# Scores of two query tiles issued in one go, and the first chunks loaded and ordered anew, in an attention and channel-mix kernel

## Chip, core and metric

The kernel runs on one core of a Trainium2 chip. The metric is device microseconds of one execution. PE is TensorE (matrix products), DVE VectorE, ACT ScalarE, POOL GpSimd, and SP SyncE, whose queue issues all DMA here.

## What is computed

Eight batches, eight heads, 576 queries, head width 64. Keys and values are mean-pooled by eight, so each head has 72 keys. The attention output, 4608 rows of 512, goes through a gated channel mix:

```python
k_p = k.reshape(B, H, Sp, pool, D).mean(axis=3)      # Sp = 72
scores = scale * np.matmul(q, k_p.transpose(0, 1, 3, 2))
attn = np.exp(scores - np.max(scores, axis=-1, keepdims=True))
attn = attn / (np.sum(attn, axis=-1, keepdims=True) + 1e-09)
x = matmul(attn, v_p)                                # heads joined: 8 x 576 x 512
xk = mu_k * x + (1.0 - mu_k) * x_prev                # x_prev: one row earlier
xr = mu_r * x + (1.0 - mu_r) * x_prev
k = np.maximum(xk @ w_k, 0.0)                        # 512 -> 1024
v = k * k @ w_v                                      # 1024 -> 512
r = 1.0 / (1.0 + np.exp(-(xr @ w_r)))
return (r * v).astype(np.float32)
```

## The kernel before

The 4608 rows are cut into 36 **tiles** of 128 queries and 13 **chunks** (128, 256, then eleven of 384 rows, three tiles each). Attention works by tile, the channel mix by chunk.

For a tile, `softmax` takes the PSUM tile `sc` (two banks; there is one such tile) and calls `part`. From tile 3 on (`ROWS_FROM`) the scores are 16 products of 64x72 with 64 rows and 64 columns of the array each (L710), so that four stand in the array side by side; each is two PE records in the profile, 32 for a tile. DVE takes the row maxima (L743) and subtracts them (L760), after which `sc` is free (`emptied`); ACT takes the exponential (L766), DVE sums, and DVE or POOL scales into `px` and `pm` (L781, L786, by the table `NORM_BY`). `transposed` (four transposes, L821) and `transposed_rest` (one, L868) turn the result, each in one bank of the kind `bank`. There are three such banks, and three of the kind `mm`.

For a chunk, `quarters` multiplies by the values (L897, L905) into `sc` and two of the kind `bank`; `shifted` and `joined` (L998) mix each row with the one before it; `x_parts` splits the result into two float32r halves (`xkh`, `xkl`, `xrh`, `xrl`: L1020 on ACT, L1022 on POOL). Then `hidden` (L1048: eight groups of 12 products of 384 columns), `gate` (L1097: three groups of 12 of 512) and `mixed` (L1130: three groups of 24 of 512) run on banks of the kind `mm`; DVE multiplies the mix by the gate (`rs`, L1140).

Chunks 0 and 1 run on whole float32 weights while the weights arrive. Each of the 20 weight blocks (eight of `w_k`, four of `w_r`, eight of `w_v`, 512 KB each) is loaded (L478) as raw 64-bit words, rebuilt into float32 by `convert` (ACT L519, DVE L521 and L524), and cut into two float32r parts by `split` (ACT L546, DVE or POOL L549). Key and value loads go through staging buffers (L502), of which the first chunks have few: `stage_103` is handed from `k0` to `v0`, `k2`, `k3`, `v3` or `v2`, and so on, each load waiting until the sums of the one before (L556, L598, L567) are done. `LOADS` is the order in which SP issues the first loads; a load that waits holds back all behind it.

No engine's order is written out by hand. Each piece of work is a generator in `Order`, with a due time plus a correction from the table `EARLIER`; while the program is built, a list scheduler with costs for each step picks the next piece, and that order is fixed in the program.

Of the kernel before, what the change touches and what calls it, by code (L numbers as in the profile page):

```python
# [38 lines left out]
WHOLE_ATT = (0, 1)  # L39
TWICE = 3  # L40
PACKED = (0, 1)
SPREAD_ON_ACT = (0, 1)
HALVED = (0,)
EARLY = (("sl", 2), ("xrl", 1))

REBASE = 2.0 ** -((1023 - 127) // 8)

LOADS = (
    "k0 wk0 c0 r1 k1 r0 q0 q2 q1 v0 wk1 v1 q5 q3 k2 wk2 wk3 q4 k3 wk4 v3 wk5 wk6 wk7 wr0 wr1 v2 wr2 "
    "wr3 wv2 wv0 wv1 wv3 wv4 wv5 wv6 wv7 "  # L50
)

SUM_BY = {"k0": "t", "k1": "v", "v0": "t", "v1": "t", "r0": "g", "k2": "g", "k3": "v", "v2": "g", "v3": "v", "r1": "v"}

NORM_BY = {0: 'g', 1: 'v', 2: 'v', 3: 'v', 4: 'g', 6: 'g', 5: 'v', 7: 'v'}
WARMING = 4
FILLERS = 40

LOW_BY = {"k": "gvgvvvgv", "r": "gvgv", "v": "gvvgvvgv"}
BY_HEAD = ((0, 1),)  # L60

ROWS_FROM = 3
BESIDE = (1,)
SQUARED_ON_ACT = (8, 0)
COPIES_ON_ACT = ()

EARLIER = {
# [42 lines left out]
}  # L110
PLAN = ""
SPARE = 0.5
# [137 lines left out]
def attention_then_channel_mix(  # L250
# [15 lines left out]
    order = Order()  # L266
    need = lambda *what: ("need", *what)
    take = lambda kind: ("take", kind)
# [82 lines left out]
    for tag, n in EARLY:  # L351
        t = sb.tile([P, n, 2 * POOL * KEYS], F32, name=f"early_{tag}", tag=tag)
# [16 lines left out]
    def stretches(at, n):  # L369
# [9 lines left out]
    tiles = [  # L379
        (c, o, stretches(a + o, P)) for c, (a, n) in enumerate(zip(starts, CHUNKS)) for o in range(0, n, P)  # L380
    ]
# [61 lines left out]
    held = {}  # L443
# [183 lines left out]
    def last_values(b):  # L627
# [34 lines left out]
        order.give("vq", vq)  # L662
        order.make(("rest", b))

    def softmax(i):

        parts = tiles[i][2]
        if i:
            yield need(("scoring", i - 1))
            c = tiles[max(i - 2, 0)][0] - 1  # L670
            if c >= 0 and c not in WHOLE_ATT:
                yield need(("attended", c, 0))
        yield need(("q", i), *[("keys", b, p) for b, *_ in parts for p in range(1 if i in HALVED else 2)])
        pair = None
        if i in BESIDE:
            pair = [(yield take("mm")), (yield take("mm"))]
            sc = None
            halves = [t.rearrange("p (a n) -> p a n", a=1) for t in pair]
        else:
            sc = yield take("sc")  # L680
            halves = [sc[:, a:a + 1] for a in range(2)]
        held["halves", i] = sc, pair, halves
        if i in HALVED:
            for kind in ("mx", "e", "sm", "px", "pm"):
                held[kind, i] = yield take(kind)
        order.make(("scoring", i))
        if i in HALVED:
            yield from part(i, 0, 1)
        else:
            yield from part(i, 0, 2)  # L690
# [3 lines left out]
            held[kind, i] = yield take(kind)  # L694
        return held[kind, i]

    def part(i, a0, a1):
        parts, na, rows = tiles[i][2], a1 - a0, i >= ROWS_FROM
        mine = slice(a0, a1)
        yield need(("scoring", i))  # L700
        sc, pair, halves = held["halves", i]
        yield need(*[("keys", b, p) for b, *_ in parts for p in range(a0, a1)])
        qs = held["q", i]
        yield "pe", 0.86 if rows else (1.0 if len(parts) == 1 else 1.14) * na / 2, False
        if rows:
            for g in range(NPAIR):
                for b, _, n, o in [(b, 0, D, o + d) for b, _, n, o in parts for d in range(0, n, D)]:
                    for a in range(2):
                        r, k = slice(a * D, (a + 1) * D), g * KEYS
# [5 lines left out]
        for g in range(2 * a0, 2 * a1) if not rows else ():  # L715
            k = (g % 2) * 2 * KEYS
            for b, _, n, o in parts:
# [1 line left out]
                    out=halves[g // 2][o:o + n, 0, k:k + 2 * KEYS],  # L719
                    lhsT=qs[:, g, o:o + n], rhs=kbd[b % 2][:, g, :], start=True, stop=True,  # L720
                )
        order.make(("scores", i, a0))

        def emptied():
            order.make(("emptied", i, a0))
            if pair:
                for a in range(a0, a1):
                    order.give("mm", pair[a])

        if na == 1:  # L730
            svs = [halves[a0]]
# [3 lines left out]
        n = 8 * KEYS // 2 * na  # L735
# [42 lines left out]
        v = NORM_BY.get(i, "g") == "v"  # L778
# [465 lines left out]
```

## Time and profile before

| | |
|---|---|
| three runs | 624.78, 624.91, 625.52 us; median 624.91 |
| the profiled execution | 624.51 us |
| its span | 622.7 us |
| PE busy | 612.5 us, 98% of the span |
| DVE, ACT, POOL busy | 59%, 56%, 34% |
| DMA queue of the loads and stores | 22.7% of 16 engines' span |

A busy share says how long an engine had at least one instruction in flight. Matrix products overlap, so PE's pace is read from the distance between two starts in the timeline rather than from a duration. The span is 1.8 us shorter than the execution's own time.

### The profile page before, as it was taken

How to read it: one execution, taken by the hardware profiler on the slowest of the kernel's cores; microseconds unless marked ns; L12 is line 12 of the kernel's file. 1: busy time of each engine (PE TensorE's matmuls, PEld its weight loads, DVE VectorE, ACT ScalarE, POOL GpSimd, SP SyncE). 2: the span in 40 equal slices, each digit the busy share in tenths (PEclk: the TensorE clock that was granted, in tenths of full speed). 3: DMA queues.
4: the chain of work that ended last, by engine and by line, in shares of the span. 5: the costliest groups of instructions: out<-in, count | busy, mean ns of one | idle time of the engine just before them, and what ended most of it. 6: DMA issues, size and time to landing. Idle time of an engine off the chain costs nothing.

```text
span 622.7 us, 10827 instructions
## 1 busy us (share of the span) xinstructions
PE 612.5 (98%) x4175; PEld 515.6 (83%) x4175; DVE 368.1 (59%) x730; ACT 351.1 (56%) x759; POOL 210.5 (34%) x333
## 2 busy tenths in 40 slices
PE   8999999999999999999999999999999999999997
PEld 7986448879879879977978978977887987987986
DVE  5999888776457366566636736737735735623411
ACT  4678847766656537636627636645654653655320
POOL 0432286066043039128216107405604303405000
PEclk9999999999999999999999999999999999999999
DMA  8467622331014211052011411033001100000001
GB/s 309 171 235 254 245 103 79 124 129 35 18 49 147 60 52 52 1 204 69 1 52 63 157 52 47 7 123 126 24 17 52 35 1 35 18 1 34 18 0 52
DMA packets 19011, 50.56 MB, mean 81 GB/s; under 512 B 2256, under 2 KB 2512, under 8 KB 18960
## 3 DMA queue, kind: packets, MB, share of 16 engines
q1 hardware_dynamic: 18960, 49.87, 22.7%
q8 instruction: 33, 0.54, 0.4%
q14 instruction: 18, 0.15, 0.1%
HBM read 40.43 MB, written 9.44 MB: 80 GB/s over the span
## 4 chain that ended last, share of the span: by engine, by line
PE 80%; DVE 6%; POOL 5%; DMA 4%; ACT 2%; issue 2%; SPq 0%; POOLq 0%; DVEq 0%; ACTq 0%
PE mm L1048 29%; PE mm L1130 24%; PE mm L1097 15%; PE sc L710 3%; PE bank L821 2%; POOL xkl L1022 2%; DMA stage<-in_kT 2%; DMA got_wv<-in_w_v 1%; PE bank L431 1%; DVE stage L556 1%; POOL xrl L1022 1%; PE sc L905 1%; DMA got_wk<-in_w_k 1%; DVE kbd L598 1%; PE mm L567 1%
## 5 line engine op out<-in xcount | busy, mean ns | idle before, releaser
L1048 PE MATMUL mm<-xkh,w_k 128*128 128x384 f32 x704 | 180.8, 337 | 2.1 <-DVE rs L1140 1.1
L1130 PE MATMUL mm<-w_v,sh 128*128 128x512 f32 x528 | 173.1, 398 | 0.0
L1048 PEld LDWEIGHTS mm<-xkh,w_k 128*128 128x128 f32 x704 | 125.9, 188 | 4.0 <-ACT xkh L1020 1.6
L1130 PEld LDWEIGHTS mm<-w_v,sh 128*128 128x128 f32 x528 | 99.1, 188 | 26.9 <-issue 5.0
L1048 PE MATMUL mm<-xkl,w_k 128*128 128x384 f32 x352 | 118.0, 335 | 0.9 <-POOL xkl L1022 0.9
L1130 PE MATMUL mm<-w_v,sl 128*128 128x512 f32 x264 | 103.3, 391 | 0.0
L781 POOL TENSOR_TENSOR px<-e,sm 128x64 f32<-128x64 f32 (+1 forms) x32 | 11.2, 350 | 261.4 <-DVE sm L775 197.7
L1097 PE MATMUL mm<-w_r,xrh 128*128 128x512 f32 x264 | 85.2, 395 | 0.0
L1073 DVE TENSOR_TENSOR sl<-rk,sh 128x384 fp32r<-128x384 f32 x88 | 54.2, 617 | 34.7 <-ACT sh L1071 34.7
L1071 ACT CAST sh<-rk 128x384 fp32r<-128x384 f32 x88 | 45.2, 514 | 47.7 <-DVE rk L1065 47.2
L1048 PEld LDWEIGHTS mm<-xkl,w_k 128*128 128x128 f32 x352 | 66.1, 188 | 1.6 <-POOL xkl L1022 1.6
L743 DVE TENSOR_REDUCE mx<-sc 128x8 f32<-128x576 f32 (+1 forms) x36 | 26.4, 735 | 57.7 <-PE sc L710 57.0
L1065 DVE SCALAR_TENSOR_TENSOR rk<-mm,rk 128x384 f32<-128x384 f32 x88 | 48.7, 553 | 17.6 <-ACT rk L1058 17.2
L1022 POOL TENSOR_TENSOR xkl<-xm,xkh 128x384 fp32r<-128x384 f32 x44 | 44.3, 1016 | 43.7 <-ACT xkh L1020 39.8
L1097 PEld LDWEIGHTS mm<-w_r,xrh 128*128 128x128 f32 x264 | 49.6, 188 | 10.2
L1130 PEld LDWEIGHTS mm<-w_v,sl 128*128 128x128 f32 x264 | 49.6, 188 | 9.3
L1058 ACT ACTIVATE rk<-mm 128x384 f32<-128x384 f32 x88 | 42.9, 489 | 22.1 <-PE mm L1048 18.9
L556 POOL TENSOR_TENSOR stage<-stage 128x512 f32<-128x512 f32 (+7 forms) x59 | 52.6, 898 | 2.2 <-DVE pr L848 0.3
L1097 PE MATMUL mm<-w_r,xrl 128*128 128x512 f32 x132 | 51.5, 390 | 0.0
L766 ACT ACTIVATE e<-e 128x576 f32<-128x576 f32 (+1 forms) x36 | 24.4, 679 | 46.4 <-DVE e L760 46.0
L1140 DVE TENSOR_TENSOR rs<-mm,rs 128x512 f32<-128x512 f32 x36 | 24.7, 685 | 41.6 <-PE mm L1130 41.5
L1022 POOL TENSOR_TENSOR xrl<-xm,xrh 128x384 fp32r<-128x384 f32 x44 | 44.4, 1019 | 0.6 <-ACT xrh L1020 0.3
(143 smaller groups left out, 909.7 us busy)
## 6 DMA issues: line engine op xcount, KB each, us to landing
qs<-in_qT SPq DMA_DIRECT2D x36, 256.0 KB, 3.1
out<-rs SPq DMA_DIRECT2D x36, 256.0 KB, 2.0
stage<-in_kT SPq DMA_DIRECT2D x15, 576.0 KB, 4.7
stage<-in_vm SPq DMA_DIRECT2D x15, 512.0 KB, 3.8
got_wk<-in_w_k SPq DMA_DIRECT2D x8, 512.0 KB, 5.3
got_wv<-in_w_v SPq DMA_DIRECT2D x8, 512.0 KB, 10.4
stage<-in_vr SPq DMA_DIRECT2D x6, 384.0 KB, 3.6
got_wr<-in_w_r SPq DMA_DIRECT2D x4, 512.0 KB, 7.5
```

The source lines that it names most:

```text
L556: nc_eng.tensor_tensor(out=st[:, :, :w], in0=st[:, :, :w], in1=st[:, :, w:2 * w], op=ALU.add)
L743: nc.vector.tensor_reduce(out=by_bank(mx)[:, o], in_=sv, axis=AX.X, op=ALU.max)
L766: nc.scalar.activation(out=e[:, mine], in_=e[:, mine], func=AF.Exp, scale=scale)
L1022: nc.gpsimd.tensor_tensor(out=lo, in0=xm[:, :n], in1=hi, op=ALU.subtract)
L1048: nc.tensor.matmul(out=hp, lhsT=w[:, o], rhs=x[:, ct, :n], start=(ct == 0 and k == 0), stop=(ct == NCT - 1 and k == len(terms) - 1),)
L1058: nc.scalar.activation(out=rk[:, :n], in_=hp, func=AF.Relu)
L1065: nc.vector.scalar_tensor_tensor(out=rk[:, :n], in0=hp, scalar=0.0, in1=rk[:, :n], op0=ALU.max, op1=ALU.mult)
L1071: nc.scalar.copy(out=sh[:, :n], in_=rk[:, :n])
L1073: nc.vector.tensor_tensor(out=operand("sl", c)[:, jt, :n], in0=rk[:, :n], in1=sh[:, :n], op=ALU.subtract)
L1097: nc.tensor.matmul(out=bank, lhsT=x[:, ct, o], rhs=w, start=(ct == 0 and k == 0), stop=(ct == NCT - 1 and k == len(terms) - 1),)
L1130: nc.tensor.matmul(out=bank, lhsT=s[:, o], rhs=w, start=(jt == 0 and k == 0), stop=(jt == NJT - 1 and k == len(terms) - 1),)
L1140: nc.vector.tensor_tensor(out=rs, in0=bank, in1=rs, op=ALU.mult)
```

## The change

Two things. First, from tile 9 on (`PAIRS_FROM`) tiles go in pairs, (9, 10), (11, 12) and so on to (33, 34), with tile 35 alone. The first of a pair takes `sc` and also two of the three tiles of the kind `bank`, waits until the tile before the pair is emptied and both query loads and all keys are there, and then issues the scores of both, the second tile's into the two banks. The second tile's `part` starts at the maxima, by bank: two maxima and two subtractions of 288 columns in place of one each of 576.

Second, `LOADS` and nearly all of `EARLIER` have new values, and some steps of the first chunks change their engine: spreading the last values (L651 on ACT to L656 on DVE), six copies of L848 to ACT, three squares from ACT to DVE, one set of sums from POOL to DVE, the norm of tile 7 from DVE to POOL.

```diff
-SPREAD_ON_ACT = (0, 1)
+SPREAD_ON_ACT = ()
 LOADS = (
-    "k0 wk0 c0 r1 k1 r0 q0 q2 q1 v0 wk1 v1 q5 q3 k2 wk2 wk3 q4 k3 wk4 v3 wk5 wk6 wk7 wr0 wr1 v2 wr2 "
-    "wr3 wv2 wv0 wv1 wv3 wv4 wv5 wv6 wv7 "
+    "k0 c0 k1 wk0 r0 q0 r1 q1 wk1 q5 wk2 v1 v0 q2 q4 wk3 k2 q3 wk4 k3 wk5 wk6 wk7 v3 wr0 wr1 wr2 wr3 "
+    "wv2 wv0 wv1 wv3 wv4 wv5 v2 wv6 wv7 "
 )
-SUM_BY = {..., "r0": "g", ..., "v2": "g", ..., "r1": "v"}
+SUM_BY = {..., "r0": "t", ..., "v2": "v", ..., "r1": "g"}
+PAIRS_FROM = 9
-SQUARED_ON_ACT = (8, 0)
-COPIES_ON_ACT = ()
+SQUARED_ON_ACT = (5, 0)
+COPIES_ON_ACT = (1, 2, 3, 4)
 EARLIER = {
-    "filling": 493.7, "last_values 1": 512.3, "convert k 0": 153.8, "split k 0": -68.2, ...
+    "filling": 417.4, "last_values 1": 487.3, "convert k 0": 480.0, "split k 0": 222.7, ...
...
+    def leads(i):
+        return i >= PAIRS_FROM and (i - PAIRS_FROM) % 2 == 0 and i + 1 < len(tiles)
     def softmax(i):
+        if leads(i - 1):
+            yield need(("scores", i, 0))
+            yield from part(i, 0, 2)
+            return
...
+        if leads(i):
+            yield need(
+                ("emptied", i - 1, 0), ("q", i + 1), *[("keys", b, p) for b, *_ in tiles[i + 1][2] for p in range(2)]
+            )
+            pair = [(yield take("bank")), (yield take("bank"))]
+            held["halves", i + 1] = None, pair, [t.rearrange("p (a n) -> p a n", a=1) for t in pair]
+            order.make(("scoring", i + 1))
...
     def part(i, a0, a1):
+        if not leads(i - 1):
...
+            scores(i, a0, a1)
+            if leads(i):
+                scores(i + 1, 0, 2)
+                order.make(("scores", i + 1, 0))
```

Three places show what this does to the order of instructions; line numbers in the changed file are 1 to 27 higher.

On PE in chunk 2, before: the scores of tiles 9 and 10 stand in `sc` one after the other, with products of the gate between them.

```order
L710 MATMUL sc_110<-kbd_68,qs_102 64x72 x16
L1097 MATMUL mm_115<-w_r_772,xrh_850 128x512
...
L821 MATMUL bank_112<-ident,pm_88 128x128 x4
...
L710 MATMUL sc_110<-kbd_68,qs_101 64x72 x16
L1097 MATMUL mm_115<-w_r_828,xrh_850 128x512
```

On PE in chunk 2, now (L721 is L710 before); the two bank rows alternate, 16 in all:

```order
L1124 MATMUL mm_116<-w_r_819,xrh_850 128x512
L721 MATMUL sc_110<-kbd_68,qs_100 64x72 x16
L721 MATMUL bank_111<-kbd_68,qs_101 64x72
L721 MATMUL bank_112<-kbd_68,qs_101 64x72
...
L1124 MATMUL mm_116<-w_r_888,xrh_850 128x512
```

The 32 products of two tiles now follow each other without anything between them.

On PE in the mix of chunks 0 and 1, before: `got_wv_667` is the seventh block of `w_v` to be rebuilt, and its first product stands behind a tile's scores and the quarters of chunk 2.

```order
L1130 MATMUL mm_115<-got_wv_641,stage_105 128x512
L710 MATMUL sc_110<-kbd_69,qs_102 64x72 x16
...
L897 MATMUL sc_110<-ptr_614,vbd_r_73 128x192 x2
...
L1130 MATMUL mm_115<-got_wv_663,stage_105 128x512
L1130 MATMUL mm_115<-got_wv_667,stage_105 128x512
```

There now (L1157 is L1130 before); the seventh block is `got_wv_703`:

```order
L1157 MATMUL mm_115<-got_wv_547,sh_478 128x512
...
L848 MATMUL bank_111<-ident,pm_88 128x128 x4
L1157 MATMUL mm_115<-got_wv_703,sh_478 128x512
L721 MATMUL sc_110<-kbd_69,qs_100 64x72 x16
L1157 MATMUL mm_115<-got_wv_708,sh_478 128x512
...
L924 MATMUL sc_110<-ptr_638,vbd_r_73 128x192 x2
```

Its first product now stands ahead of those scores and of the quarters.

On SP's queue, before: `v2` (the first row here) stands ahead of two `w_r` and all eight `w_v` blocks.

```order
L502 DMA stage_103<-in_vm 128x1024
L478 DMA got_wr_619<-in_w_r 128x1024
L478 DMA got_wr_627<-in_w_r 128x1024
L478 DMA got_wv_635<-in_w_v 128x1024
...
L478 DMA got_wv_676<-in_w_v 128x1024
```

There now (L503 and L479 are L502 and L478 before):

```order
L479 DMA got_wv_540<-in_w_v 128x1024
L479 DMA got_wv_547<-in_w_v 128x1024
L503 DMA stage_103<-in_vm 128x1024
L479 DMA got_wv_703<-in_w_v 128x1024
L479 DMA got_wv_708<-in_w_v 128x1024
```

Only the seventh and eighth block stand behind it now.

## Rows read from the trace of the kernel before

**Rows 1.** The page: busy time and share of the span, and the clock in 40 slices
```profile
PE 612.5 (98%) x4175; PEld 515.6 (83%) x4175; DVE 368.1 (59%) x730; ACT 351.1 (56%) x759; POOL 210.5 (34%) x333
...
PEclk9999999999999999999999999999999999999999
```

**Rows 2.** Busy time by stretch, us (instructions), for the whole program
```profile
0.00:95.50 95.50, 91.75 (x637) 67.18 (x637) 78.47 (x174) 65.46 (x158) 38.38 (x70) 1.00 0.60 215
95.50:600.00 504.50, 501.84 (x3457) 433.14 (x3458) 287.58 (x554) 284.57 (x600) 172.11 (x264) 1.00 0.17 58
```

**Rows 3.** Waits of PE: line and tile, waited for: us in total, times, longest
```profile
PE mm L1048 <- DVE rs L1140: 1.1, 1, 1.1
PE mm L1048 <- ACT xkh L1020: 1.0, 2, 0.5
PE mm L1048 <- POOL xkl L1022: 0.9, 2, 0.5
PE sc L718 <- ACT e L752: 0.7, 1, 0.7
PE bank L821 <- DVE xm L998: 0.5, 1, 0.5
```

**Rows 4.** Timeline of PE round one tile's scores: start us, us, instruction
```profile
169.83 0.39 PE L1097 MATMUL mm<-w_r,xrl 128*128 128x512 f32 x1
170.06 0.39 PE L1097 MATMUL mm<-w_r,xrh 128*128 128x512 f32 x1
170.38 0.73 PE L710 MATMUL sc<-kbd,qs 64*64 64x72 f32 x32
171.04 0.50 PE L1130 MATMUL mm<-w_v,sh 128*128 128x512 f32 x1
171.38 0.40 PE L1130 MATMUL mm<-w_v,sl 128*128 128x512 f32 x1
```

**Rows 5.** The same scores seen through two narrower windows
```profile
170.56 0.56 PE L710 MATMUL sc<-kbd,qs 64*64 64x72 f32 x24
...
170.87 0.24 PE L710 MATMUL sc<-kbd,qs 64*64 64x72 f32 x4
```

**Rows 6.** Timeline of PE round the four transposes of one tile
```profile
184.27 0.39 PE L1130 MATMUL mm<-w_v,sh 128*128 128x512 f32 x1
184.50 0.60 PE L821 MATMUL bank<-ident,pm 128*128 128x128 f32 x4
...
185.17 0.40 PE L1130 MATMUL mm<-w_v,sl 128*128 128x512 f32 x1
```

**Rows 7.** Groups of DVE by form: xcount | busy us, mean ns | idle before
```profile
L760 DVE TENSOR_TENSOR e<-sc,mx 128x576 f32<-128x576 f32 x34 | 25.7, 755 | 1.2
...
L743 DVE TENSOR_REDUCE mx<-sc 128x8 f32<-128x576 f32 x34 | 25.5, 751 | 57.1 <-PE sc L710 57.0
...
L743 DVE TENSOR_REDUCE mx<-mm 128x4 f32<-128x288 f32 x2 | 0.9, 449 | 0.0
L760 DVE TENSOR_TENSOR e<-mm,mx 128x288 f32<-128x288 f32 x2 | 0.9, 435 | 0.0
```

**Rows 8.** Timeline of DVE: the conversions of the seventh and eighth w_v blocks
```profile
72.96 1.28 DVE L524 SCALAR_TENSOR_TENSOR got_wv<-got_wv,tmp 128x512 int32<-128x512 int32 x2
```

**Rows 9.** Timeline of PE: quarters of chunk 2, then w_v blocks five to eight
```profile
72.13 0.77 PE L897 MATMUL sc<-ptr,vbd_r 96*128 96x192 f32 x2
...
75.29 3.70 PE L1130 MATMUL mm<-got_wv,stage 128*128 128x512 f32 x8
```

**Rows 10.** SyncE's queue: start us, us, the loads
```profile
50.18 0.33 SPq L502 DMA_DIRECT2D stage<-in_vm  x1
...
51.50 6.31 SPq L478 DMA_DIRECT2D got_wv<-in_w_v  x8
```

**Rows 11.** Loads: size and median us to landing
```profile
got_wk<-in_w_k SPq DMA_DIRECT2D x8, 512.0 KB, 5.3
got_wv<-in_w_v SPq DMA_DIRECT2D x8, 512.0 KB, 10.4
```

More of the change, by code (lines that the diff above doesn't have):

```diff
@@ L48 @@
 LOADS = (
-    "k0 wk0 c0 r1 k1 r0 q0 q2 q1 v0 wk1 v1 q5 q3 k2 wk2 wk3 q4 k3 wk4 v3 wk5 wk6 wk7 wr0 wr1 v2 wr2 "
-    "wr3 wv2 wv0 wv1 wv3 wv4 wv5 wv6 wv7 "
-)
-SUM_BY = {"k0": "t", "k1": "v", "v0": "t", "v1": "t", "r0": "g", "k2": "g", "k3": "v", "v2": "g", "v3": "v", "r1": "v"}
-NORM_BY = {0: 'g', 1: 'v', 2: 'v', 3: 'v', 4: 'g', 6: 'g', 5: 'v', 7: 'v'}
+    "k0 c0 k1 wk0 r0 q0 r1 q1 wk1 q5 wk2 v1 v0 q2 q4 wk3 k2 q3 wk4 k3 wk5 wk6 wk7 v3 wr0 wr1 wr2 wr3 "
+    "wv2 wv0 wv1 wv3 wv4 wv5 v2 wv6 wv7 "
+)
+SUM_BY = {"k0": "t", "k1": "v", "v0": "t", "v1": "t", "r0": "t", "k2": "g", "k3": "v", "v2": "v", "v3": "v", "r1": "g"}
+NORM_BY = {0: 'g', 1: 'v', 2: 'v', 3: 'v', 4: 'g', 6: 'g', 5: 'v'}
 WARMING = 4
 FILLERS = 40
-LOW_BY = {"k": "gvgvvvgv", "r": "gvgv", "v": "gvvgvvgv"}
+LOW_BY = {"k": "gvgvvvgv", "r": "gvgv", "v": "gvvvgggv"}
 BY_HEAD = ((0, 1),)
 ROWS_FROM = 3
+PAIRS_FROM = 9
 BESIDE = (1,)
-SQUARED_ON_ACT = (8, 0)
-COPIES_ON_ACT = ()
+SQUARED_ON_ACT = (5, 0)
+COPIES_ON_ACT = (1, 2, 3, 4)
 EARLIER = {
[42 rows of a table removed]
[14 rows of a table added]
+    "warm": 494.6, "constants": 228.5, "complements": 181.3, "loads": 66.6, "keys 0 0": 471.9,
[27 rows of a table added]
 }
@@ L663, in last_values @@
         order.make(("rest", b))
+    def leads(i):
+        return i >= PAIRS_FROM and (i - PAIRS_FROM) % 2 == 0 and i + 1 < len(tiles)
     def softmax(i):
         parts = tiles[i][2]
+        if leads(i - 1):
+            yield need(("scores", i, 0))
+            yield from part(i, 0, 2)
+            return
+        group = [i, i + 1] if leads(i) else [i]
         if i:
             yield need(("scoring", i - 1))
-            c = tiles[max(i - 2, 0)][0] - 1
+            c = tiles[max(group[-1] - 2, 0)][0] - 1
             if c >= 0 and c not in WHOLE_ATT:
@@ L695, in shared, with scores @@
         return held[kind, i]
[L697 to L704, printed above, removed]
+    def scores(i, a0, a1):
+        parts, halves, qs = tiles[i][2], held["halves", i][2], held["q", i]
+        rows = i >= ROWS_FROM
         if rows:
@@ L721, in part @@
                 )
-        order.make(("scores", i, a0))
+    def part(i, a0, a1):
+        parts, na, rows = tiles[i][2], a1 - a0, i >= ROWS_FROM
+        mine = slice(a0, a1)
+        yield need(("scoring", i))
+        sc, pair, halves = held["halves", i]
+        if not leads(i - 1):
+            yield need(*[("keys", b, p) for b, *_ in parts for p in range(a0, a1)])
+            if rows:
+                yield "pe", 1.365 if leads(i) else 0.865, False
+            else:
+                yield "pe", (1.0 if len(parts) == 1 else 1.14) * na / 2, False
+            scores(i, a0, a1)
+            if leads(i):
+                scores(i + 1, 0, 2)
+                order.make(("scores", i + 1, 0))
+            order.make(("scores", i, a0))
         def emptied():
@@ L727, in emptied @@
                 for a in range(a0, a1):
-                    order.give("mm", pair[a])
+                    order.give("mm" if i in BESIDE else "bank", pair[a])
         if na == 1:
```

83 rows, old and new, of the table EARLIER are left out of this document.

## Prediction

> **What bounds the kernel now.** I read the page first. PE is busy for 612.5 of 622.7 us and its clock is at the full 2.4 GHz level in all 40 slices [rows 1]; no other engine comes near. Then the stretches: in the first 95.5 us PE is busy 91.75 us and DVE 78.47 us with 174 instructions, so there DVE is a second bound; from 95.5 to 600 us PE is busy 501.84 of 504.5 us, and DVE little more than half [rows 2]. Then PE's waits: in the first 95.5 us 1.1 us for the multiplication by the gate, which frees a bank of the kind `mm`, and 0.7 us for the first scores; later 2.4 us in five waits (1.0, 0.9 and 0.5) [rows 3]. So nearly nothing is to be had from waits. What PE does must become shorter, or the order in which it does it cheaper, and the question for each wait is only whether a new one appears.
>
> **What a tile's scores cost PE.** The steady distance of two float32r products of 512 columns is 0.23 us (169.83 to 170.06). Round a tile's scores the last product of the gate starts at 170.06 and the second of the mix at 171.38: 1.32 us, of which two distances of 0.227 belong to the products themselves. The scores take the other 0.87 us [rows 4]. How much of that grows with their number? Seen through two windows, 24 of the 32 records start from 170.56 on and the last 4 from 170.87 on, so 20 records take 0.31 us, 15.6 ns each, and 32 take 0.50 us [rows 5]. The remaining 0.37 us are paid once for the group, before the first and behind the last record: the first scores start 0.32 us after the product ahead of them, not 0.23, and the second product behind them 0.34 us after the first [rows 4].
>
> Is the 0.37 us a price of float32, or of the small array tiles? The four transposes of a tile, also float32 but on the whole array, answer that. From 184.27 to 185.17 are 0.90 us; without two distances 0.45 us are left, and 0.35 of these pass between the start of the first transpose and that of the next product, 184.50 to 184.85 [rows 6]. At most 0.1 us is paid at their ends. It is therefore the change between the whole array and its quarters that costs 0.37 us, once for each group.
>
> **Pairs: the main term.** Tiles 9 to 34 make 13 pairs. In each, 0.37 us is paid once and not twice; the records themselves keep their 0.50 us for a tile, since the 32 of the second tile alternate between two banks as those of the first do. 13 x 0.366 = 4.8 us. All other PE instructions are the same in kind and number, so this is all that PE's pace gains. The ends of this term: nothing, if a change of PSUM banks costs what a change of array does; within `sc` each four records already go to two banks at 15.6 ns, so I stay at the upper end.
>
> **Pairs: what they add on DVE, and who waits.** The second tile has two maxima and two subtractions of 288 columns, 0.449 and 0.435 us each, for one of each of 576 columns at 0.751 and 0.755 us [rows 7]: 1.77 us for 1.51, or 0.26 us a pair, 3.4 us in all on an engine that is idle for over 200 us behind 95.5 us; I cost it at nothing. For its cover: the pair's banks are emptied after 0.75 + 0.76 + 2 x 0.45 + 2 x 0.44, about 3.3 us. The first instructions on PE that want one of them are, in four pairs, the quarters of the next chunk, behind 24 products of the mix, 24 x 0.227 = 5.4 us. Cover 2.1 us; in the other pairs the distance is larger. If DVE is late by more than that, PE waits for the excess there.
>
> The Trainium skill, page "TensorEngine Tiling (Array Packing)", section "PSUM Bottleneck", speaks against such a change: it says that cutting the array speeds up the products but not the emptying of PSUM, which can then become the bottleneck. The trace of before does not bear it out here: 3.3 us of emptying stand against 5.4 us until the next use. By that rule the sum would lose what exceeds the cover, by the rows nothing.
>
> **First chunks: weights and DVE.** The seventh block of `w_v` is rebuilt on DVE at 72.96 to about 73.6 (two instructions in 1.28 us) [rows 8]. PE first needs it as the third block of those from 75.29 on, eight records in 3.70 us, so about 77.0 [rows 9]. Slack 3.4 us. In the new order 146 DVE instructions stand ahead of that conversion, 145 before; DVE is there at about the same time. PE is earlier: it no longer has the quarters of chunk 2 (72.13 to 75.29, 3.2 us [rows 9]), one tile's scores (0.87) and one product of 0.86 us (two records) ahead of it, 4.9 us in all. 3.4 - 4.9 is a new wait of 1.5 us. Against it stands the wait of 1.1 us [rows 3], which I take as gone: in the new order chunk 2's first products start on a bank whose mix ended a tile's scores and three float32 products earlier, some 3.4 us, and the multiplication that frees it is one DVE instruction. The net is +0.4 us. The ends: -1.8 us, if the earlier weights also take away the two waits of the first stretch and the new one does not come; +4.0 us, by the load of `v2`. Before, it was issued at 50.18 and the blocks behind it from 51.50 on [rows 10]. Now it waits for sums of `v3` that end behind 126 DVE instructions, 20 ahead of the conversion; at 78.47 / 174 = 0.45 us each [rows 2] that is 9 us ahead of it, about 64.6. A load takes 5.3 us alone and 10.4 in a queue of eight [rows 11]; a burst of three is nearer the first, which lands at about 70 and is covered. The second would land at 75, be rebuilt about 77 and cost PE up to 5.1 us, less the 1.1.
>
> What moves between ACT, DVE and POOL in the first chunks is in those counts. The remaining waits (2.4 us later on) I leave as they are: the scheduler places the same work by the same rules, and others of that size will come.
>
> **Sum.** -4.8 + 0.4 = -4.4 us. The profiled execution took 624.51 us, 1.8 us more than its span; it stands 0.4 us under the median of 624.91, from which the prediction counts: **620.5 us**.
>
> **Rivals.**
> 1. Banks come free late: DVE reaches the second tile's maxima over 2 us late because sums of keys or a multiplication by the gate stand ahead. Each microsecond of excess at the four places costs 4 us in all: 624.5. For it: only three such banks exist. Against: `sc` had the same distance to the quarters before, and no wait of PE for L760 is among the rows [rows 3]. This is the outcome that the section "PSUM Bottleneck" of the Trainium skill's page "TensorEngine Tiling (Array Packing)" would expect.
> 2. The pair does not save what it should, because the change of banks is paid again: 625.
> 3. Slower: the queue of the first chunks. If `v2`'s slot, and with it the seventh and eighth block, comes late, PE stands at their first product with all of chunk 2 behind it. It decides from 6 us of wait on (4.8 saved, 1.2 beyond): conversion at about 78 where it was 73.6. Then 626.5. For it: SP issues in order, and one staging buffer serves `k2`, `k3`, `v3` and `v2` in turn. Against: six of the eight blocks no longer stand behind `v2`.
> 4. The first chunks gain: earlier blocks let DVE run ahead, and all waits of the first stretch go: 618.
>
> **How the numbers follow.** Forecast 0.62, its own range 618.3 (both early waits gone) to 622.3 (half of the first chunks' upper end); rival 4 0.12; rival 1 0.09; rival 2 0.05; rival 3 0.07; the first chunks losing 2 to 4 us without deciding 0.05. A measurement of this kernel can tell 0.2%, 1.25 us, from no change. Faster by more than that: 0.62 + 0.12 + 0.05 = 0.79; within it rivals 1 and 2, 0.14; slower 0.07. The range reaches from 617.5 (rival 4 with a little of the later 2.4 us) to 624.1 (624.91 - 4.8 + 4.0), and leaves out rivals 2 and 3 and part of rival 1.
>
> **What would show it.** Right: from tile 3 on PE's scores stand in 20 groups (seven single tiles, 13 pairs) where there were 33, a pair costing about 1.37 us (from the last product ahead to the second behind, less two distances); PE busy some 4 to 5 us shorter; no wait of PE at the quarters for DVE's subtraction. The new wait, of about 1.5 us, on a `w_v` block between 68 and 76 us, and the wait for the gate's multiplication near 94 us gone. Wrong: a pair that takes 1.7 us, PE waits on the banks behind each pair, or PE resuming chunk 2 later than 95.5 us by several microseconds.

## The result, and the profile after

The changed kernel took **619.98 us** (median of 4 runs, 619.57 to 620.45) beside 625.05 us for the kernel before on the same chip (4 runs, 624.78 to 625.52): a ratio of 0.9918, 95% interval 0.9901 to 0.9936. It is 5.1 us faster. The forecast was 620.5 us, the range 617.5 to 624.1. A second set, shown below, gave 620.44 us against 624.97 us.

The page of the changed kernel (its parts 1 and 2, as [rows 1]):

```profile
span 617.8 us, 10866 instructions
PE 606.2 (98%) x4175; PEld 515.2 (83%) x4175; DVE 363.5 (59%) x757; ACT 356.9 (58%) x760; POOL 211.4 (34%) x333
PEclk9999999999999999999999999999999999999999
```

The clock is at its 2.4 GHz level throughout, as it was, and PE is busy 6.3 us less with the same number of matmuls. To see where the 4.9 us of span went, both programs are cut at the same work: the start of the 24th of the 48 product records of the mix of chunks 0 and 1 (81.0 and 79.9 us), and of the 48th of 72 in the mix of chunk 2 (136.2 and 135.7 us) and of chunk 12, the last (613.0 and 608.1 us). Busy time by these stretches (length, then PE, PEld, DVE, ACT, POOL, clock, DMA), first before, then after:

```profile
0.00:81.00 81.00, 78.39 (x569) 60.51 (x570) 65.70 (x156) 57.63 (x140) 24.64 (x51) 1.00 0.65 236
81.00:136.20 55.20, 54.06 (x368) 41.72 (x367) 46.48 (x85) 36.90 (x75) 28.98 (x38) 1.00 0.33 113
136.20:613.00 476.80, 474.14 (x3216) 408.87 (x3215) 254.56 (x489) 256.57 (x546) 156.87 (x246) 1.00 0.15 52
```

```profile
0.00:79.90 79.90, 77.49 (x569) 60.50 (x570) 65.68 (x157) 54.69 (x131) 18.89 (x39) 1.00 0.65 240
79.90:135.70 55.80, 53.68 (x368) 41.53 (x367) 45.09 (x87) 38.38 (x80) 34.13 (x49) 1.00 0.34 112
135.70:608.10 472.40, 469.19 (x3217) 408.72 (x3217) 251.31 (x513) 263.81 (x551) 158.39 (x246) 1.00 0.15 52
```

The PE instructions of a stretch are the same in kind and number to within one, so the lengths can be compared. The first stretch became 1.1 us shorter, the second 0.6 us longer (one pair lies in it), and the third, with the other 12 pairs, 4.4 us shorter. Call the change of PE from the whole array to its quarters and back a passage: twelve at 0.366 us are 4.4 us. Nearly all of the gain lies where the pairs lie.

Waits of PE in the changed kernel (as [rows 3]):

```profile
PE bank L895 <- DVE xm L1025: 2.5, 3, 1.4
PE sc L721 <- DVE xm L1025: 1.6, 1, 1.6
PE bank L422 <- DVE tmp L418: 1.5, 1, 1.5
PE mm L1075 <- DVE rk L1092: 1.2, 2, 1.0
PE bank L895 <- ACT tmp L520: 0.4, 1, 0.4
PE bank L848 <- DVE pm L813: 0.2, 1, 0.2
PE mm L1157 <- DVE got_wv L525: 0.2, 1, 0.2
```

Apart from the wait of the first instruction (L422, as in the kernel before), these are 6.1 us, against 4.4 us in the kernel before. L721 is the scores' matmul, L895 the transposition of `pr`, L1025 the product that makes `xm`, L1075 the hidden products, L1157 the mix. No wait is for a subtraction of scores (L787), which empties a pair's banks.

So the waits grew by 1.7 us and the span still became 4.9 us shorter: 6.6 us less pass between PE's starts where nothing waits. Thirteen passages are 4.8 of them. The other 1.8 us (1.0 up to 135.7 us, 0.8 behind) lie neither in the pairs nor in the waits. The profile of this kernel's second set has the same 1.8 us; the run with seven pairs, in the same order up to the 23rd tile, has none of it. No run here isolates it.

One pair on PE, away from every wait (start, length, instruction; single tile: [rows 4]):

```profile
189.71 0.39 PE L1157 MATMUL mm<-w_v,sh 128*128 128x512 f32 x1
190.03 0.73 PE L721 MATMUL sc<-kbd,qs 64*64 64x72 f32 x32
190.58 0.68 PE L721 MATMUL bank<-kbd,qs 64*64 64x72 f32 x32
191.19 0.62 PE L1075 MATMUL mm<-xkh,w_k 128*128 128x384 f32 x2
```

The first tile's scores start 0.32 us behind the product ahead of them, as in [rows 4]. The second tile's follow 0.55 us later, near the 0.50 us that their records alone were priced at: no second passage. From the last product ahead to the second one behind, less two steady distances, the ten plain pairs cost 1.363 to 1.369 us. A single tile costs 0.866 us in the kernel before (0.864 at the one plain place left in this trace), so two cost 1.732. The difference is 0.366 us.

### The profile page after: what moved, and what is told of

Same layout as the page of the kernel before. It is cut to its first block, busy times and chain, and to the rows that moved or that the text cites. A ratio compares the mean times of both kernels' runs of the same rounds, so it can differ in the third digit from the quotient of the medians.

```text
span 617.8 us, 10866 instructions
## 1 busy us (share of the span) xinstructions
PE 606.2 (98%) x4175; PEld 515.2 (83%) x4175; DVE 363.5 (59%) x757; ACT 356.9 (58%) x760; POOL 211.4 (34%) x333
## 4 chain that ended last, share of the span: by engine, by line
PE 80%; POOL 6%; DVE 5%; ACT 4%; issue 2%; DMA 2%; SPq 0%; POOLq 0%; ACTq 0%; DVEq 0%
PE mm L1075 28%; PE mm L1157 26%; PE mm L1124 16%; PE bank L848 2%; POOL xkl L1049 2%; DMA got_wv<-in_w_v 2%; POOL xrl L1049 2%; PE sc L721 1%; PE sc L932 1%; POOL stage L557 1%; PE bank L932 1%; DVE xm L1025 1%; PE bank L721 1%; PE bank L432 1%; PE sc L924 1%
## 5 line engine op out<-in xcount | busy, mean ns | idle before, releaser
L1075 PE MATMUL mm<-xkh,w_k 128*128 128x384 f32 x704 | 181.6, 338 | 1.2 <-DVE rk L1092 1.2
L1157 PE MATMUL mm<-w_v,sh 128*128 128x512 f32 x528 | 170.5, 395 | 0.0
L1075 PEld LDWEIGHTS mm<-xkh,w_k 128*128 128x128 f32 x704 | 125.9, 188 | 3.8 <-DVE rk L1092 2.6
L1157 PEld LDWEIGHTS mm<-w_v,sh 128*128 128x128 f32 x528 | 99.1, 188 | 25.9 <-issue 5.0
L1075 PE MATMUL mm<-xkl,w_k 128*128 128x384 f32 x352 | 117.8, 335 | 0.0
L1157 PE MATMUL mm<-w_v,sl 128*128 128x512 f32 x264 | 102.9, 390 | 0.0
L808 POOL TENSOR_TENSOR px<-e,sm 128x64 f32<-128x64 f32 (+1 forms) x33 | 13.0, 395 | 214.5 <-DVE sm L802 199.0
L1075 PEld LDWEIGHTS mm<-xkl,w_k 128*128 128x128 f32 x352 | 66.1, 188 | 0.0
L1157 PEld LDWEIGHTS mm<-w_v,sl 128*128 128x128 f32 x264 | 49.6, 188 | 9.6
L1025 DVE SCALAR_TENSOR_TENSOR xm<-sc,given,t 128x384 f32<-128x384 f32 x44 | 25.5, 613 | 46.1 <-ACT t L984 32.0
L557 POOL TENSOR_TENSOR stage<-stage 128x512 f32<-128x512 f32 (+7 forms) x56 | 48.5, 871 | 6.2 <-DVE rk L1092 2.9
L984 ACT ACTIVATE t<-sc,om_sb 128x384 f32<-128x384 f32 x44 | 22.0, 584 | 44.8 <-PE sc L932 44.8
```

The costliest lines, as they stand in the source:

```text
L557: nc_eng.tensor_tensor(out=st[:, :, :w], in0=st[:, :, :w], in1=st[:, :, w:2 * w], op=ALU.add)
L984: nc.scalar.activation(out=ts[m][:, 1:n + 1], in_=xp, func=AF.Copy, scale=om_sb[:, m, g:g + 1])
L1025: nc.vector.scalar_tensor_tensor(out=xm[:, :n], in0=bank[:, :n], scalar=mu_sb[:, m, g:g + 1], in1=ts, op0=ALU.mult, op1=ALU.add,)
L1075: nc.tensor.matmul(out=hp, lhsT=w[:, o], rhs=x[:, ct, :n], start=(ct == 0 and k == 0), stop=(ct == NCT - 1 and k == len(terms) - 1),)
L1157: nc.tensor.matmul(out=bank, lhsT=s[:, o], rhs=w, start=(jt == 0 and k == 0), stop=(jt == NJT - 1 and k == len(terms) - 1),)
```

## The experiments

All times are medians. The kernel before ran beside each set on the same chip, and comparisons go by the ratio to it.

**Pairs and settings apart.** Is the gain in the pairs or in the new loads, tables and due dates? Each was taken alone as far as the scheduler finds an order: with the new settings and no pair at all it finds none, so one pair stays.

```
-PAIRS_FROM = 9
+PAIRS = (9,)
 def leads(i):
-    return i >= PAIRS_FROM and (i - PAIRS_FROM) % 2 == 0 and i + 1 < len(tiles)
+    return i in PAIRS
```

> The changed kernel with all its new settings, loads and due dates, but one pair alone (tiles 9 and 10); the other 24 tiles are single again. Theory (the gain is the pairs, 0.366 us each; the new settings are worth about nothing): 620.0 + 12 x 0.366 = 624.4 us, so no faster than the kernel before by more than 1 us. Rival (the new settings carry the gain): 620 to 621 us.

It took 625.57 us against 625.63: 0.9997 (0.9988 to 1.0006). The other way round, the kernel before with its own `LOADS`, `EARLIER`, `SUM_BY`, `NORM_BY`, `LOW_BY`, `SPREAD_ON_ACT`, `SQUARED_ON_ACT` and `COPIES_ON_ACT`, and only the code of the pairs:

> The kernel before with its own loads, due dates and tables, with the code of the pairs alone and pairs from the tenth tile on. Theory: 13 x 0.366 = 4.8 us below the kernel before, 620.3 us; the order made with the old due dates may add a wait or two of PE, up to 2 us, since banks are taken in pairs. Rival (without the new due dates the pairs' two banks stall the transpositions and the attended sums): 625 us or more, waits of PE for ACT or DVE at the banks of over 5 us in all.

622.52 us against 625.63: 0.9954 (0.9942 to 0.9967), 2.9 us faster where 4.8 were expected. In its trace a plain pair costs what it costs in the changed kernel (1.82 us from the last product of the gate to the second of the mix in both), so the pairs gain the same; what is missing against the forecast is in the waits:

```profile
PE mm L1075 <- DVE rk L1092: 2.1, 3, 1.1
PE bank L895 <- DVE xm L1025: 1.9, 2, 1.4
PE sc L721 <- DMA qs<-in_qT: 0.8, 1, 0.8
```

With five smaller ones they are 7.1 us, 2.7 us more than in the kernel before, and -4.8 + 2.7 = -2.1 us; the profiled execution's span is 2.0 us shorter than before's. So with one pair the new settings gain nothing, and with all pairs they are worth some 2 us (0.9954 against 0.9918). Of the 2.9 us between the two profiled spans (620.7 and 617.8) only 1.0 are fewer waits; the rest are the unplaced 1.8 us above. The rival that the settings carry the gain is out.

**Fewer pairs.** The same edit with `PAIRS = tuple(range(9, 22, 2))`.

> The changed kernel with 7 pairs (tiles 9 to 22) and 12 single tiles from 23 on, everything ahead of the 23rd tile's scores in the same order as in the changed kernel. Theory (0.366 us a pair): 620.0 + 6 x 0.366 = 622.2 us, and the last product of the middle of the program comes later by as much. Rival (the gain lies in the first chunks): 620.0 us. Rival (late pairs collide with something at the end): below 620.

622.55 us against 625.62: 0.9952 (0.9939 to 0.9965), so 2.1 us more than the changed kernel's 0.9918 would be on this chip; expected were 2.2, so both rivals are out. Singles from tile 23 on cost 1.32 us from product to product at the places where pairs cost 1.82.

**The passage by itself.** What does a pair save: a passage of PE from the whole array to its quarters and back, or something else? A transposition of the identity, a product on the whole array, was put between the two tiles of each pair, and in a control ahead of both. The order is that of the changed kernel in both.

```
 scores(i, a0, a1)
 if leads(i):
+    nc.tensor.transpose(out=held["halves", i + 1][1][0][:, :P], in_=ident, identity=ident)
     scores(i + 1, 0, 2)
```

> The changed kernel in its own order, with one transposition of the identity (a product on the whole array, into the second tile's bank, overwritten by its scores) between the two tiles' scores of each of the 13 pairs. Theory (what a pair saves is one passage from the whole array to the small tiles and back): 13 x (0.366 + 0.111) = +6.2 us over the changed kernel, 626.2 us, and a pair's visit takes 1.366 + 0.477 = 1.843 us. Rival (the saving is of another kind: adjacent banks, or one wait fewer): only the transposition's own 13 x 0.111 = 1.4 us, 621.4 us.

> The control of the run with the transposition between: the same transposition, but ahead of both tiles' scores, so that no passage is added. Theory and rival: 13 x 0.111 = +1.4 us, 621.4 us; the difference of the two runs, divided by 13, is the price of one passage to the small tiles and back (theory 0.366 us, rival 0).

The same pair as above, first with the transposition between, then ahead:

```profile
191.21 0.39 PE L1158 MATMUL mm<-w_v,sh 128*128 128x512 f32 x1
191.53 0.73 PE L721 MATMUL sc<-kbd,qs 64*64 64x72 f32 x32
192.19 0.33 PE L747 MATMUL bank<-ident 128*128 128x128 f32 x1
192.45 0.73 PE L721 MATMUL bank<-kbd,qs 64*64 64x72 f32 x32
193.11 0.62 PE L1076 MATMUL mm<-xkh,w_k 128*128 128x384 f32 x2
```

```profile
192.06 0.39 PE L1159 MATMUL mm<-w_v,sh 128*128 128x512 f32 x1
192.29 0.27 PE L746 MATMUL bank<-ident 128*128 128x128 f32 x1
192.49 0.73 PE L721 MATMUL sc<-kbd,qs 64*64 64x72 f32 x32
193.04 0.68 PE L721 MATMUL bank<-kbd,qs 64*64 64x72 f32 x32
193.66 0.61 PE L1077 MATMUL mm<-xkh,w_k 128*128 128x384 f32 x2
```

From the last product ahead to the first behind: 1.48 us without the transposition, 1.60 with it ahead, 1.90 with it between. The transposition costs 0.11-0.12, and 0.31 us more if it interrupts the quarters (0.31 to 0.32 at all 13 pairs). It is float32 like the scores, so what is paid is not a change of number format. So the passage is what a pair saves, and the rival is out. Its price is not one number: 0.366 us between wide products, 0.31 round a single transposition.

The totals follow less well: 624.41 us (0.9981, 0.9972 to 0.9990) and 621.92 us (0.9939, 0.9927 to 0.9952). The first is about 3.9 us above the changed kernel by the ratios, where the theory had 6.2 and the rival 1.4. The places give 13 x 0.31 = 4.1 us between the two runs, the medians 2.5 us. In the two profiled executions, 2.3 us apart, a reason is seen: the control waits 2.1 us for `sc` at 87.6 us, the other run 0.8 us, and the control then loses 1.7 us to the clock (last section). What the other executions lost there is not known. Single places are therefore the better measure here, and totals only confirm sign and rough size.

**A pair's banks without the shared visit.** The two tiles of a pair were made two steps of the order again, in the same banks.

```
 if leads(i - 1):
-    yield need(("scores", i, 0))
+    yield need(("scores", i - 1, 0))
     yield from part(i, 0, 2)
     return
...
-    scores(i, a0, a1)
-    if leads(i):
-        scores(i + 1, 0, 2)
-        order.make(("scores", i + 1, 0))
+    scores(i, a0, a1)
```

> The changed kernel with its settings, loads and banks, but the scores of a pair's two tiles are two steps of the order again, with other products between them where the order puts them. Theory (the 13 shared visits to the small tiles are the gain, 0.366 us each): 620.0 + 13 x 0.366 = 624.8 us; each visit costs 0.866 us again. Rival (the gain comes from the first chunks' new settings, or from the second tile having banks of its own): 620 to 621 us.

640.67 us against 625.62: 1.0246 (1.0225 to 1.0267). Both theories miss this: 15.9 us more than the one predicted. The waits say what came in:

```profile
PE mm L1071 <- POOL xkl L1045: 4.8, 10, 0.6
PE mm L1071 <- ACT xkh L1043: 4.5, 4, 2.2
PE bank L891 <- ACT pth L851: 1.8, 2, 1.6
```

The hidden products wait for the parts of `xm`, because the attended sums come late. In the changed kernel the sums of chunks 5 to 11 start 14.4 to 16.0 us before the chunk's first hidden product; here four of the seven start less than 8 us before it (7.8, 5.7, 7.3 and 6.2). Chunk 5 shows how. The scores of its tile 14 come at 209.20, 18 us behind those of tile 13 (191.11), where the changed kernel has both at 190; and the sums, which need `sc` and two of the three banks of the kind `bank`, start at 234.2, behind the scores of tile 16 (230.64), which stand in two such banks that were taken with tile 15's scores at 224.27. So a late second tile and banks held for long act together, and the run does not tell them apart. It suggests that the first rival, banks that come free late, lies close by, and that the pair escapes it by filling its banks at once. In the profiled execution the waits come to 10.0 us more than in the changed kernel, and the clock falls twice behind them (last section). The run gives no price of the passage, since everything behind is ordered anew.

**More pairs.** `PAIRS_FROM = 3`.

> The changed kernel with pairs from the fourth tile on: 16 pairs in place of 13, no single visits but the one of the last tile. Theory: three passages fewer, 3 x 0.366 = 1.1 us below the changed kernel, 618.9 us, if the first chunks' order holds. Rival (the first chunks are set by loads and by DVE, and a pair takes two banks there): no gain or slower, 620 to 623 us, with new waits of PE ahead of 100 us.

645.92 us against 625.63: 1.0334 (1.0319 to 1.0348). The rival, and far worse than it said. The longest wait of PE, and busy time during it and behind it:

```profile
PE bank L848 <- DVE pr L877: 13.5, 1, 13.5
```

```profile
83.70:97.20 13.50, 0.00 (x1) 0.03 (x1) 12.24 (x27) 3.66 (x5) 4.38 (x5) 0.61 0.56 185
97.20:108.00 10.80, 7.88 (x50) 5.36 (x50) 1.99 (x5) 5.13 (x13) 2.28 (x8) 0.50 0.00 0
```

It is not the banks that PE waits for here: behind a pair's scores at 82.47 the next instruction on PE is the transposition of a tile's weights, and no other product is placed between. DVE is busy for 12.24 of the 13.5 us with both tiles' maxima, subtractions and sums and with keys that it adds up. Among the first chunks PE has no other work ahead to cover two softmaxes, and DVE is the second bound there [rows 2]. Then the clock is at its 1.2 GHz level (0.50 up to 108.0 us, 0.51 from there to 117.6) and makes the next stretch longer too.

**One visit for two sequences' sums.** If a passage costs 0.3 us or more anywhere, the attended sums of a chunk that lies in two sequences pay it twice: whole array, quarters, whole array, quarters. The second sequence's products were put in the opposite order, with the start of its accumulation on the quarters.

```
-for b, s, k, at in units[c]:
-    for g in range(NPAIR):
+def on_whole(n, b, k, at):
+    for g in range(NPAIR):
...
-            rhs=operand("ptr", c)[:, g // 2, at:at + k], start=True, stop=False,
+            rhs=operand("ptr", c)[:, g // 2, at:at + k], start=(n == 0), stop=(n > 0),
...
-    for a in range(2):
+def on_quarters(n, b, k, at):
+    for a in range(2):
...
-                rhs=operand("pth", c)[rows, g, at:at + k], start=False, stop=True,
+                rhs=operand("pth", c)[rows, g, at:at + k], start=(n > 0), stop=(n == 0),
...
+for n, (b, s, k, at) in enumerate(units[c]):
+    for do in (on_quarters, on_whole) if n else (on_whole, on_quarters):
+        do(n, b, k, at)
```

> The changed kernel, and in the chunks that lie in two sequences the second sequence's attended sums in the opposite order (the products on the quarters of the array first, then those on the whole array), so that the quarters of both sequences are one visit. Theory (a passage from the whole array to small tiles and back costs 0.31 to 0.37 us wherever it is): each of these four chunks' sums takes 0.31 to 0.37 us less, 3.32 to about 2.98 us from the product ahead to the second behind, and the kernel 1.2 to 1.5 us less, 618.6 us. Rival (the passage is free where the whole array's products are short ones of 192 or 384 columns): no change, 620.0 us.

619.70 us against 625.63: 0.9903 (0.9889 to 0.9916). In the three later such chunks the sums take 2.99 us from the product ahead to the second behind, where the changed kernel has 3.32: 0.33 us, as expected (in chunk 2, among float32 weights, 3.39 in place of 3.73). The sums of chunk 5 and the mix round them, in the changed kernel and then in this run (L1163 is L1157):

```profile
223.93 0.39 PE L1157 MATMUL mm<-w_v,sh 128*128 128x512 f32 x1
...
227.25 0.39 PE L1157 MATMUL mm<-w_v,sl 128*128 128x512 f32 x1
```

```profile
223.94 0.39 PE L1163 MATMUL mm<-w_v,sh 128*128 128x512 f32 x1
...
226.93 0.40 PE L1163 MATMUL mm<-w_v,sl 128*128 128x512 f32 x1
```

The rival is out. The interval of the total overlaps that of the changed kernel, so it was measured again beside it.

> The changed kernel again, as it is, beside the next run on the same chip: 620.0 us; its ratio to the kernel before 0.992.

> The run with one visit for both sequences' sums again, beside the changed kernel on the same chip. Theory: 4 x 0.33 = 1.3 us below the changed kernel, 618.7 us. Rival (the gain of the first time was the spread of the runs): 620 us.

620.44 us (0.9927, 0.9914 to 0.9940) and 618.48 us (0.9900, 0.9884 to 0.9915), against 624.97. The order of the two is as expected, and the intervals touch at their ends. On the same chip, with one more pair and 18 due dates moved:

```
-PAIRS_FROM = 9
+PAIRS_FROM = 7
-"transposed 7": 260.8, "quarters 3": 182.1, "attended 2 3": 41.4,
+"transposed 7": -55.9, "quarters 3": 38.5, "attended 2 3": -106.5, "softmax 9": -60,
...
```

> One visit for both sequences' sums as in the run before, 14 pairs (from the eighth tile on), and the due dates of 18 steps of the second and third chunk moved so that the order has the banks for the earlier pair. Theory: one passage fewer than the run with 13 pairs and one visit, and no new wait: 619.7 - 0.4 = 619.3 us, and a little less where waits of PE for DVE at the banks go as well. Rival (a pair in the third chunk holds two of three banks while the first chunks' sums need them, as 16 pairs did): 620 to 625 us, with a wait of PE between 75 and 110 us.

617.83 us, 0.9897 (0.9878 to 0.9917), and not the rival's 620 to 625: the fastest of all, with 5.1 us of waits besides the first where the changed kernel had 6.1. Over the run with one visit the 0.6 us are within the spread; over the kernel before the gain is 7.1 us.

## Why the prediction was right, and where it was off

**The main term held in size.** 13 x 0.366 = 4.8 us: the plain pairs cost 1.366 us as worked out, the 12 pairs behind 135.7 us take 4.4 us out of their stretch, and 12 more pairs with the same settings are worth 0.9997 - 0.9918 = 0.8%, 4.9 us. The waits of that stretch grew by 0.8 us (2.4 in [rows 3]; 3.2 after, of which 2.0 for `xm` at L895 and 1.2 for `rk`), so it gained another 0.8 us that I did not place. The scores stand in 20 groups, as forecast; PE's busy time fell by 6.3 us and not by 4 to 5: the span fell by 4.9 us and PE's idle time in it grew by 1.4.

**The step from float32 to the array** (the transposes of [rows 6] pay nearly nothing, so it is the quarters that cost) is now shown, not only argued, by the transposition put between. The Trainium skill, page "TensorEngine Tiling (Array Packing)", section "Key Properties", has a sentence on this: "Changing tiling mode (not just tile) drains the TensorE". The traces agree that such a change costs time, at 0.31 to 0.37 us for a visit; the section gives no price.

**Rival 2** (the change of banks is paid again) is out: 0.55 us from the first to the second tile's scores. **Rival 1** did not come true in the changed kernel, where no wait is for L787, nor did what the section "PSUM Bottleneck" of the Trainium skill's page "TensorEngine Tiling (Array Packing)" warns of. The run that pulls a pair's two tiles apart, at 1.0246, shows what late second tiles and banks held for long can do together.

**The first chunks: the term of +0.4 us was mis-sized.** The step that failed was that DVE reaches the seventh `w_v` block "at about the same time" as before, 72.96 to 73.6, so that PE waits 1.5 us there. PE and DVE of the changed kernel there:

```profile
71.17 1.03 PE L1157 MATMUL mm<-got_wv,sh 128*128 128x512 f32 x2
72.14 0.73 PE L721 MATMUL sc<-kbd,qs 64*64 64x72 f32 x32
73.03 0.70 PE L1157 MATMUL mm<-got_wv,sh 128*128 128x512 f32 x1 [0.15 <-DVE got_wv L525]
86.31 0.73 PE L721 MATMUL sc<-kbd,qs 64*64 64x72 f32 x32 [1.57 <-DVE xm L1025]
```

```profile
69.88 0.43 DVE L522 TENSOR_SCALAR tmp<-tmp 128x512 int32<-128x512 int32 x1 [0.96 <-ACT tmp L520]
70.34 0.69 DVE L525 SCALAR_TENSOR_TENSOR got_wv<-got_wv,tmp 128x512 int32<-128x512 int32 x1
72.28 0.69 DVE L525 SCALAR_TENSOR_TENSOR got_wv<-got_wv,tmp 128x512 int32<-128x512 int32 x1
```

DVE rebuilt the seventh block by 71.0, 2.6 us earlier than I had it, and PE began on it at 71.2, right behind; the eighth was ready at 73.0 and cost PE 0.15 us. I had counted the instructions ahead of the conversion (146 for 145) as if each took as long as before: DVE was busy for 58.2 us ahead of it where it had been 60.1, and idle for 12.1 us where it had been 12.8. So 0.2 us stand in place of the 1.5. The upper end of the term did not come either: `v2` was issued at 64.01 (I had 64.6), and the two blocks behind it landed at 68.72 and 70.98. The 1.1 us for the multiplication by the gate went, as forecast, and so did the 0.7 us of the first scores. In their place came what I had put down only as "others of that size will come": 1.57 us of the scores at 86.31 for `sc`, which DVE's `xm` empties, 0.55 us at L895, and smaller ones.

Up to 135.7 us the waits are thus 2.9 us where they were 2.0, which alone would be more than the +0.4. Yet PE is 0.5 us earlier there than before, of which the first pair is 0.37: the first chunks are worth about -0.1 us, by the 1.0 us between starts that nothing waits for and that I did not forecast. That is most of the 0.5 us between the forecast and the median. The nearness of the total is therefore in part luck: over the whole program the waits grew by 1.7 us where the sum had 0.4, and 1.8 us less elsewhere, of which the sum had nothing, made up for it.

In the ranges, half of the first chunks' upper end gives 624.91 - 4.8 + 2.0 = 622.1, not 622.3; nothing else hangs on it.

**Rival 3** did not come near: PE waited 0.2 us in all for blocks of `w_v`. **Rival 4** came half: the two waits of the first stretch went, and others came.

## What to carry to other kernels

Price a visit to small tiles as a fixed part and a part that grows with its products, from two windows on one group in the trace; then look for all places where the array changes its tiling, and join those that are due near each other, as the pairs did and as the sums of two sequences did after them. The price of joining is in the buffers and in the cover: the run that pulls the tiles apart suggests filling the banks of two tiles at once, and the one with 16 pairs shows that the engine needs other work while both are emptied. The new settings were worth nothing with one pair and some 2 us with all, so settings are to be judged with the change that they serve. And a total that comes out as forecast does not prove each of its terms: hold the waits and the stretches against the sum as well.

## What the runs showed of the hardware

A somewhat longer stop of PE went with a loss larger than the time it added. In nine profiles of the same place, the scores at about 86 us wait for `sc`; in eight of them 0.39 to 1.57 us, and the six products behind take 2.84 us. In the run with the transposition ahead they waited 2.09 us:

```profile
87.61 0.73 PE L721 MATMUL sc<-kbd,qs 64*64 64x72 f32 x32 [2.09 <-DVE xm L1027]
88.28 4.54 PE L1159 MATMUL mm<-got_wv,stage 128*128 128x512 f32 x6
```

```profile
87.60:92.60 5.00, 4.99 (x38) 2.42 (x39) 3.31 (x6) 3.92 (x8) 4.56 (x11) 0.66 0.16 58
```

The same six products took 4.54 us: the granted clock was 0.66 on average over 87.6 to 92.6 us, a mix of its two levels, and 1.00 again behind. Half a microsecond more of waiting went with 1.7 us more for the same products. The run with the two tiles of a pair apart shows such a fall twice. Its hidden products wait 2.20 us at 394.57; at 445.52 and 447.23 two stops of 1.24 and 1.41 us follow each other closely. The wait, and what came behind each (the granted clock is the third figure from the end):

```profile
394.57 0.62 PE L1071 MATMUL mm<-xkh,w_k 128*128 128x384 f32 x2 [2.20 <-ACT xkh L1043]
```

```profile
396.00:400.00 4.00, 4.00 (x16) 4.00 (x15) 1.11 (x2) 1.51 (x5) 3.84 (x5) 0.57 0.00 0
400.00:405.00 5.00, 5.00 (x31) 5.00 (x30) 3.15 (x7) 2.77 (x8) 2.11 (x3) 1.00 0.00 0
447.00:451.00 4.00, 3.40 (x10) 2.75 (x11) 1.30 (x3) 3.67 (x10) 3.70 (x4) 0.58 0.17 63
```

Single stops of up to 1.67 us elsewhere in the profiles were not followed by such a fall. So three places, and the 13.5 us stop above behind which the clock was 0.50, speak for the stops as the cause; no run changed the length of a stop by itself.

The price of a visit to the quarters depends on what lies round it: 0.366 us between products of 384 and 512 columns, 0.33 between the attended sums' products of 192, 0.31 round one transposition of 128. Which property of the neighbours sets it was not tried.
